# Retention and a two-layer GELU network on one core: seven products for half of the first layer in blocks 3 to 6, scans on GpSimd, attention work in the second layer, the last block by halves

## The chip, the cores and the metric

The kernel runs on one core of one Trainium2 chip. The time is that of one execution on the device, in microseconds (us); of several runs the median is given. A profiled execution comes with it, which has a time of its own.

The core has four engines that compute, each with its own queue of instructions, worked off in order: TensorE (PE; its weight loads are PEld and lie under the matmuls), VectorE (DVE), ScalarE (ACT) and GpSimd (POOL). SyncE (SP) has the queue from which nearly all transfers start. Engines wait for each other through semaphores.

## The reference

Inputs are `q`, `k`, `v` of 8 batches, 8 heads, 576 positions and 64 values a head, and the weights `w_in` (512 x 2048) and `w_out` (2048 x 512), all float32.

```python
def _attn_ref(q, k, v):
    scores = scale * np.matmul(q, k.transpose(0, 1, 3, 2))
    Dmat = np.where(rel >= 0, gamma[:, None, None] ** rel[None, :, :], 0.0)
    return np.matmul(scores * Dmat[None], v)

def _moe_ref(x, w_in, w_out):          # x: 4608 tokens of 512
    h = x @ w_in
    g = 0.5 * h * (1.0 + np.tanh(c * (h + 0.044715 * h * h * h)))
    return g @ w_out
```

Here `gamma` is one decay for each head and `rel` the distance of two positions. The heads of one position, side by side, are one token of the second function.

## The kernel before, in words

**Attention.** A batch's 576 positions are four chunks of 128 and a tail of 64. Tails of two batches are worked on as a pair. Inside a chunk the scores are multiplied by a mask (`score`, then `masks` on DVE) and by v (`av`). What earlier chunks contribute goes through a state: `state` makes a chunk's k-v products in PSUM, `scan` adds them to the state so far and multiplies by a decay (two DVE operations, the first without the addition), `spread` copies the result as float16 into a tile that `past` multiplies with q (`tbd` for chunks, `tbt` for tails). `put` copies a finished chunk from PSUM into `xT`, the network's input.

**Network.** Tokens go in nine blocks of 512, numbered 0 to 8: blocks 0 to 7 are the chunks of one batch each, block 8 holds all the tails. While block t is in the network, the attention of batch t+1 is computed and, from `xT`, block t+1 is built. Batches 0 to 2 are turned by TensorE; from batch 3 on (`NPE = 3`) POOL scales and casts q and k (`cast`), and a DMA transposes them.

A block has a first layer (`up`: 16 plain tiles, each four matmuls of 512 columns, then a GELU on ACT into `gT`) and a second layer. The second layer is done, from block 1 on, as a two-by-two product with **seven products** instead of eight: `prod(t, m, u)` is product m (1 to 7) for half u of the tokens, 8 matmuls of 256 columns. It needs sums of activations (`act_sums`, on DVE, both inputs in SBUF) and of weights (`weight_sums`, made once). `after(t, m, u)` combines products on DVE and stores them. They stand in the order 1, 6, 5, 7, 2, 4, 3, each with two halves; products that share a bank of PSUM (`opA`, `opB`, `opC`) wait until the one before is read. Product 4 writes `opB` after product 7's add has read it.

In blocks 7 and 8 (`WIN`) three quarters of the first layer also go by seven products. `up_prod(t, j, m)` is product m of group j, four matmuls of 256 columns; a group stands for four plain tiles. Its results are copied or added on ACT and DVE before the GELU. `in_sums` makes sums of `w_in` for a group (four DVE operations, in block 6), `x_sums` sums of a block's tokens (four DVE operations). `W_ORDER` is the order of the steps: "12" is product 2 of group 1, "p" a plain tile, "a" activation sums, "Q" product 1 of the second layer. The seventh of a group, say "07", waits for ACT's copy of the sixth.

**Order.** It is written out by hand. A block is a row of steps, numbered u; `at(t, u, f)` puts f behind step u of block t. Steps 0 to 15 are the first layer, 16 to 29 the second. `put`, `scan`, casts and loads hang on such places. A place sets the order in each engine's queue, and nothing else.

**Loads** go to a ring of 16 buffers of 256 KB (`ld`, `LD`). A cast frees a buffer and `pump` then issues the next load of a fixed list. From step 16 of a block until step 29 loads are held back. `gate` is a small POOL copy that waits for the last activation sum, so that POOL's casts begin behind it. `lt` are three buffers of their own for the tails.

## Time and profile before

| | us |
|---|---|
| median of 3 runs | 296.65 (296.27 to 297.05) |
| profiled execution | 296.39 |
| its span | 294.7 |
| PE busy | 282.2 (96%) |
| DVE busy | 191.7 (65%) |
| ACT busy | 168.4 (57%) |
| POOL busy | 100.2 (34%) |

The granted TensorE clock has a mean of 0.997. The span runs from the first instruction to the last; the slices in the profile cut it into 40 equal parts of 7.4 us and give the busy share of each in tenths. In a line of a timeline stand the start in us, the length in us, the engine, the line of the kernel, the operation, output and inputs by name, the shapes, and how many operations are merged; in brackets the idle time before and what ended it. Matmuls are pipelined, so the mean of one (379 ns for 512 columns) is longer than the distance from one to the next. The lengths of single operations also overlap a little on the other engines.

### The profile page before, as it was taken

The page shows a single profiled execution, that of the slowest core. Times are in us where ns is not written, and L with a number is a line of the kernel's source. Part 1 is how long each engine was busy: PE and PEld are TensorE (multiplying, and loading weights), DVE is VectorE, ACT ScalarE, POOL GpSimd, SP SyncE. Part 2 cuts the span into 40 slices and gives each one's busy share as a digit, 9 for nine tenths or more (in the row PEclk, how much of TensorE's full clock was granted, in tenths as well). Part 3 has the DMA queues.
Part 4 walks back from the last instruction along what each step waited for, and adds up shares of the span by engine and source line. Part 5 has one row for each costly group of instructions (what it writes and reads, how often), then busy time and mean ns, then how long its engine had stood idle before and what let it go on. Part 6 is the DMA issues. An engine that isn't in the chain of part 4 may idle for free. (4 is left out here: it accounts for less than half of the span.)

```text
span 294.7 us, 7531 instructions
## 1 busy us (share of the span) xinstructions
PE 282.2 (96%) x3100; PEld 204.3 (69%) x3100; DVE 191.7 (65%) x396; ACT 168.4 (57%) x313; POOL 100.2 (34%) x133
## 2 busy tenths in 40 slices
PE   6779999999999999999999999999999999999993
PEld 2458745888884588448844885478547887887782
DVE  6790606789754873477448654855488968974863
ACT  5377443998239663866386736664666258507800
POOL 4587487960880082007700640059030000000000
PEclk9999999999999999999999999999999999999998
DMA  7999999999969998999899949944941030003013
GB/s 202 307 357 372 341 317 292 280 280 211 194 165 232 216 225 169 261 214 194 103 271 221 169 88 273 211 109 76 263 93 38 0 145 1 2 20 125 1 38 107
DMA packets 129058, 52.92 MB, mean 180 GB/s; under 512 B 101632, under 2 KB 120576, under 8 KB 129024
## 3 DMA queue, kind: packets, MB, share of 16 engines
q1 hardware_dynamic: 128544, 51.92, 74.5%
q8 instruction: 24, 0.39, 0.6%
q10 hardware_dynamic: 480, 0.52, 0.6%
q14 instruction: 10, 0.08, 0.1%
HBM read 36.70 MB, written 9.44 MB: 157 GB/s over the span
## 5 line engine op out<-in xcount | busy, mean ns | idle before, releaser
L471 PE MATMUL hp<-xT,w_in_sb 128*128 128x512 f16 x352 | 79.0, 379 | 0.0
L477 ACT ACTIVATE gT<-hp 128x512 f16<-128x512 f32 x88 | 50.6, 597 | 31.0 <-PE hp L471 30.4
L471 PEld LDWEIGHTS <-w_in_sb 128*128 128x128 f16 x352 | 34.0, 98 | 38.2
L666 PEld LDWEIGHTS <-gT 128*128 128x128 f16 x512 | 49.0, 98 | 7.2 <-issue 0.5
L666 PEld LDWEIGHTS <-s 128*128 128x128 f16 x384 | 37.1, 98 | 4.8
L645 DVE TENSOR_TENSOR s<-gT 128x512 f16<-128x512 f16 x32 | 14.4, 449 | 28.0 <-ACT gT L477 27.0
L953 POOL COPY gate<-s 128x1 f16<-128x1 f16 x5 | 0.9, 190 | 90.7 <-DVE s L649 90.7
L489 PE MATMUL hp<-xT,w_in_sb 128*128 128x256 f16 x256 | 30.3, 273 | 1.1 <-POOL w_in_sb L745 0.9
L666 PE MATMUL opA<-w_out_sb,gT 128*128 128x256 f16 x256 | 31.0, 273 | 0.1
L425 ACT CAST tbd<-ws 64x256 f16<-64x256 f32 x48 | 19.4, 405 | 16.0 <-DVE ws L416 15.4
L489 PEld LDWEIGHTS <-w_in_sb 128*128 128x128 f16 x256 | 24.5, 98 | 4.9 <-POOL w_in_sb L745 1.6
L666 PE MATMUL opB<-wt,gT 128*128 128x256 f16 x224 | 26.9, 273 | 0.1
L383 DVE TENSOR_TENSOR ret<-st,cm 128x512 f16<-128x512 f32 x40 | 24.8, 681 | 0.0
L266 POOL TENSOR_TENSOR cq<-ld,sc 128x512 f16<-128x512 f32 x20 | 21.7, 1086 | 0.0
L460 ACT CAST xT<-xs 128x512 f16<-128x512 f32 x36 | 19.3, 592 | 3.3 <-PE xs L450 1.8
L266 POOL TENSOR_TENSOR ck<-ld,sc 128x512 f16<-128x512 f32 x20 | 21.0, 1050 | 0.0
L495 ACT ACTIVATE gT<-hp 128x512 f16<-128x512 f32 x32 | 18.5, 602 | 3.8 <-PE hp L489 3.5
L680 DVE TENSOR_TENSOR k<-k,opB 128x512 f32<-128x512 f32 x16 | 11.0, 687 | 14.2 <-ACT k L696 7.5
L711 ACT COPY ost<-opA 128x512 f32<-128x512 f32 x8 | 4.7, 586 | 24.1 <-PE opA L666 17.5
L293 ACT COPY tt<-tr 128x1024 f16<-128x1024 f16 (+1 forms) x12 | 11.8, 998 | 10.8 <-PE tr L287 10.7
L416 DVE TENSOR_TENSOR ws<-vs,gt 128x256 f32<-128x256 f32 x24 | 15.7, 654 | 1.1
L666 PE MATMUL opC<-wt,s 128*128 128x256 f16 x128 | 15.5, 273 | 0.0
(124 smaller groups left out, 440.0 us busy)
## 6 DMA issues: line engine op xcount, KB each, us to landing
ld<-in_q_dram SPq DMA_DIRECT2D x32, 256.0 KB, 5.3
ld<-in_k_dram SPq DMA_DIRECT2D x32, 256.0 KB, 5.3
ld<-in_v_dram SPq DMA_DIRECT2D x32, 256.0 KB, 5.4
out_dram<-ost SPq DMA_DIRECT2D x16, 512.0 KB, 3.8
ld<-in_moe_w_in_dram SPq DMA_DIRECT2D x16, 256.0 KB, 5.9
ld<-in_moe_w_out_dram SPq DMA_DIRECT2D x16, 256.0 KB, 5.3
lt<-in_k_dram SPq DMA_DIRECT2D x8, 128.0 KB, 5.4
lt<-in_q_dram SPq DMA_DIRECT2D x8, 128.0 KB, 4.3
```

Of the source, the lines that this page charges most:

```text
L266: eng.tensor_tensor(out=dst.rearrange("p (h d) -> p h d", d=D), in0=raw.rearrange("p (h d) -> p h d", d=D), in1=sc[:, s0].unsqueeze(2).to_ ...
L293: cp(out=o, in_=t)
L383: nc.vector.tensor_tensor(out=r.rearrange("p (n i) -> p n i", i=128), in0=t.rearrange("p (n i) -> p n i", i=128), in1=(cm if b < PAIR else ...
L416: nc.vector.tensor_tensor(out=w, in0=uc, in1=gt, op=ALU.mult)
L425: cp(out=(tbd[b % 2][r, c, :, r] if c < NC - 1 else tbt[b % NT4][r, :, r]), in_=w[r])
L460: nc.scalar.copy(out=xT[:, g0 : g0 + 2], in_=xs.rearrange("p (n g t) -> p g n t", n=HP, g=2))
L471: nc.tensor.matmul(hp.rearrange("p (g t) -> p g t", t=TL), w_in_sb[:, ct, 128 * fc : 128 * fc + 128], xT[:, o : o + TB // TL, ct, :], star ...
L477: nc.scalar.activation(out=gT[t][:, fc].rearrange("p i n -> p (i n)"), in_=hp, func=AF.Gelu_apprx_tanh)
L489: nc.tensor.matmul(hp[:, 256 * x : 256 * x + 256].rearrange("p (g t) -> p g t", t=TL), w_in_sb[:, ct, 128 * (f + x) : 128 * (f + x) + 128] ...
L495: nc.scalar.activation(out=gT[t][:, f : f + 2, 2 * u : 2 * u + 2, :].rearrange("p f i n -> p f (i n)"), in_=hp.rearrange("p (f n) -> p f n ...
L645: nc.vector.tensor_tensor(out=s["1"], in0=a21, in1=a22, op=ALU.add)
L666: nc.tensor.matmul(op[tag][:, HD * u : HD * u + HD], lhs(f), rhs[:, f], start=(new and f == 0), stop=(f == NH - 1), skip_group_check=True,)
```

## The change

- **Blocks 3 to 6:** groups 0 and 1 of the first layer, half of it, go by seven products; `WIN` is 2 there. The other half stays plain. The order of steps is a new entry of `W_ORDER`. Two groups of `in_sums` move from block 6 to block 2; `x_sums` for the next block stands behind step 28.
- **Scans:** from batch 3 on, `take` copies the state from PSUM to SBUF on ACT, and `scan` and `spread` run on POOL, at other places.
- **Scores and masks** of blocks 3 to 6 stand in the second layer: behind steps 16 and 21 instead of 9 and 19; the tails' behind 7 and 11.
- **Last block:** both halves of product 4, then of product 2, then products 6, 5, 7, 3 for the first half of the tokens and again for the second, each with its own banks and adds of 256 columns (`prod_last`, `after_last`). Each half of the tokens is stored as it is done.
- **Memory:** the ring has 18 buffers, of which 7 are kept for sums once batch 2 is loaded; temporaries share the tags of the second layer's. The first weight sum, `wt["1"]`, is written over its own input and moves to block 1.
- **Activation sums** are cut into three parts instead of two, so that they can be placed apart. The hold on loads begins one cast later.

```diff
-    LD = 16
+    LD = 18
+    KEPT = 7
...
+        if b == NPE - 1:
+            seq += [("keep",)] * KEPT
...
+    def take(b, *cs):
+        a = att[b]
+        us = a["U", cs[0]][0]
+        t = sb.tile([128, 512], F32, tag="uc", name="uc", bufs=2)
+        nc.scalar.copy(out=t, in_=us)
+        drop(us)
+        for n, c in enumerate(cs):
+            a["U", c] = (t, n, False)
+
-    def scan(b, c):
+    def scan(b, c, eng=None):
+        eng = eng or nc.vector
...
-            nc.vector.tensor_tensor(out=s, in0=uc, in1=a["w"], op=ALU.add)
+            eng.tensor_tensor(out=s, in0=uc, in1=a["w"], op=ALU.add)
...
-        nc.vector.tensor_tensor(out=w, in0=uc, in1=gt, op=ALU.mult)
+        eng.tensor_tensor(out=w, in0=uc, in1=gt, op=ALU.mult)
...
-    WIN = {t: 3 for t in (NTB - 2, NTB - 1)}
+    FIN = (NTB - 2, NTB - 1)
+    WIN = {t: 3 if t in FIN else 2 for t in range(NPE, NTB)}
...
+    wt["1"] = W12
...
+    def prod_last(t, m, u, lhs, rhs):
+        tag = {6: "B", 7: "B", 5: "C", 3: "E"}[m] + str(u)
+        new = tag not in op
+        if new:
+            op[tag] = bank("op" + tag)
+        for f in range(NH):
+            nc.tensor.matmul(op[tag][:, 0:HD], lhs(f), rhs[:, f], start=(new and f == 0), stop=(f == NH - 1), skip_group_check=True)
+
+    def after_last(m, u):
...
+        elif m == 6:
...
+            add(keep["u2"][:, u], keep["s1"][:, u], acc("B"))
+            if u == 0:
+                for f in range(0, NH, 2):
+                    act_sums(NTB - 1, f, f + 2, parts=(2,))
+            add(keep["u3"][u][:, 0], keep["s1"][:, u], half("D"))
...
+        elif m == 5:
+            add(keep["u3"][u][:, 1], keep["s1"][:, u], acc("C"))
+            add(keep["u2"][:, u], keep["u2"][:, u], acc("C"))
+            drop(op.pop(f"C{u}"))
+        elif m == 7:
+            add(
+                keep["o1"][:, u].rearrange("p (c d) -> p c d", c=2), keep["u3"][u],
+                acc("B").unsqueeze(1).to_broadcast([128, 2, HD]),
+            )
+            drop(op.pop(f"B{u}"))
+            store(keep["o1"][:, u], 1)
+            if u == 1:
+                store(keep["o0"][:, u], 0, slice(0, HD))
+        else:
+            add(keep["o0"][:, u, HD:DM], keep["u2"][:, u], acc("E"))
+            drop(op.pop(f"E{u}"))
+            store(keep["o0"][:, u], 0, slice(0 if u == 0 else HD, DM))
...
     def later(b, c):
-        scan(b, c)
-        spread(b, c, A.copy)
+        eng = P if b >= NPE else V
+        scan(b, c, eng)
+        spread(b, c, P.tensor_copy if b >= NPE else A.copy)
...
-    W_ORDER = (
-        "01 02 05 11 06 12 p 15 07 16 21 22 p 04 25 17 03 26 14 p 13 27 p Q0 24 a0 23 a1 Q1 a3 a2"
-    ).replace("p", "").split(" ")
-    for n in range(GW):
-        at(NTB - 3, 17 + 2 * n, lambda n=n: in_sums(n, (3, 2)))
-        at(NTB - 3, 18 + 2 * n, lambda n=n: in_sums(n, (4, 1)))
-    at(NTB - 3, 27, lambda: x_sums(NTB - 2))
-    at(NTB - 2, 17, lambda: x_sums(NTB - 1))
+    W_ORDER = {
+        2: "01 02 p 05 06 p 11 07 12 p 15 16 04 p 03 17 p a2 b2 p 14 13 a0 b0 p p a1 b1 a3 b3",
+        3: "01 02 05 11 06 12 p 15 07 16 21 22 p 04 25 17 03 26 14 p 13 27 p Q0 24 c0 23 c1 Q1 c3 c2",
+    }
+    for j, (t, u) in enumerate([(NPE - 1, 17), (NPE - 1, 21), (NTB - 3, 24)]):
+        at(t, u, lambda j=j: in_sums(j, (3, 2)))
+        at(t, u if t > NPE else u + 1, lambda j=j: in_sums(j, (4, 1)))
+    for t in WIN:
+        at(t - 1, 17 if t == NTB - 1 else 28, lambda t=t: x_sums(t))
...
+        if t in WIN and t not in FIN:
+            if tl is not None:
+                at(t, 7, lambda t=t, tl=tl: scores(NTB, 0, tl))
+                at(t, 11, lambda t=t, tl=tl: outs(NTB, 0, tl))
+            at(t, 16, lambda t=t, b=b: (scores(t, 0), state(b, 2, 3), take(b, 2, 3)))
+            at(t, 17, lambda b=b: later(b, 2))
+            at(t, 20, lambda t=t: outs(t, 0))
+            at(t, 21, lambda t=t: scores(t, 2))
+            at(t, 26, lambda t=t, nb=b + 1: outs(t, 2, None, (nb, 0, 1) if nb < B else None))
+            at(t + 1, 2, lambda b=b: later(b, 3))
+            for c in range(2 if b + 1 < B else 0):
+                at(t + 1, 4 + 2 * c, lambda c=c, nb=b + 1: later(nb, c))
+            continue
...
-        at(t0, ut[0], lambda: q_ld.update(hold=True))
...
+            if (key, c) == ent[0]:
+                at(t0, u, lambda: q_ld.update(hold=True))
...
+            if t == NTB - 1:
+                two = [(4, 0), (4, 1), (2, 0), (2, 1)] + [(m, u) for u in range(2) for m in (6, 5, 7, 3)]
```

## The prediction

> **What bounds the kernel now.** I read the slices first, then the busy time of each block, then TensorE's timeline inside one block, then the other engines' timelines where the change puts work. The slices say which engine has no air:
>
> ```profile
> PE   6779999999999999999999999999999999999993
> DVE  6790606789754873477448654855488968974863
> ACT  5377443998239663866386736664666258507800
> POOL 4587487960880082007700640059030000000000
> ```
>
> PE is at 9 from the fourth slice to the last but one. Cut at the starts of blocks 2 to 8 (read off PE's timeline):
>
> ```profile
> 87.06:117.61 30.55, 30.55 (x310) 20.94 (x308) 18.93 (x38) 18.75 (x36) 8.98 (x10) 1.00 1.03 214
> 117.61:147.49 29.88, 29.88 (x286) 20.19 (x284) 17.83 (x36) 17.84 (x34) 10.58 (x11) 1.00 0.97 193
> 207.92:238.38 30.46, 30.37 (x295) 20.65 (x293) 24.18 (x53) 16.68 (x32) 2.50 (x2) 1.00 0.34 84
> ```
>
> The columns are the stretch, its length, then busy time of PE, weight loads, DVE, ACT and POOL, then clock and DMA. PE is busy for all of a block, at full clock, so a matmul that goes is time that goes, and a wait that comes is time that comes. The price of both kinds of first-layer step stands in the chain of block 7, which already has the seven products:
>
> ```profile
> 240.72 0.44 PE hA L561 x4
> 241.16 0.86 PE hp L471 x4
> ```
>
> A plain tile (four matmuls of 512 columns) is 0.865 us, a product (four of 256) 0.437. The third thing to see is what DVE pays for an operation with both inputs in SBUF while POOL runs:
>
> ```profile
> 59.32 1.27 DVE L645 TENSOR_TENSOR s<-gT 128x512 f16<-128x512 f16 x1
> 60.62 1.15 DVE L646 TENSOR_TENSOR s<-s,gT 128x512 f16<-128x512 f16 x1
> 61.70 0.83 DVE L647 TENSOR_TENSOR gT<-gT 128x512 f16<-128x512 f16 x1
> 62.45 0.83 DVE L649 TENSOR_TENSOR s<-gT,s 128x512 f16<-128x512 f16 x1
> ```
> ```profile
> 59.08 2.42 POOL L258 TENSOR_TENSOR ck<-ld,sc 128x512 f16<-128x512 f32 x2
> 61.45 1.56 POOL L255 CAST cv<-ld 128x512 f16<-128x512 f32 x2
> ```
>
> Each DVE operation ends where a POOL operation ends: the four take 3.96 us (59.32 to 63.28). With POOL idle the same four take 1.46 (64.27 to 65.83). Operations that read PSUM do not pay: the masks of block 2, in the middle of POOL's casts, stay at 0.6 us each.
>
> **The change part by part.** *Products in blocks 3 to 6.* Each block drops 8 plain tiles (8 x 0.865 = 6.92 us) and gains 14 products (14 x 0.437 = 6.12): 0.80 a block, **-3.2 us** over four. Weight loads stay under the matmuls (98 ns against 109). New beside them, per block: ACT copies of PSUM, 4 x 0.58; DVE, 8 x 0.69 to combine and 4 x 0.42 for the token sums; the GELUs keep their number.
>
> *Scans to POOL.* From batch 3 on, DVE loses 7 operations a batch (3.8 us in block 3), ACT loses 8 spreads (3.3 us) and gains two 0.59 us copies that bring the state to SBUF. DVE goes from 17.8 to about 21.2 us of some 29, ACT from 17.8 to about 18.3, POOL from 8.5 to about 14.5 (its halves of 1.04 and 0.60 us, an estimate). In sum nobody overtakes PE; waits are then a matter of place.
>
> *Block 2: eight weight sums among the casts.* Twelve weight sums stood in block 6, where POOL was idle. Eight of them now stand in block 2's second layer, where POOL makes eight casts of 1.04 us. The first four fall in a gap: DVE has finished the activation sums at 104.1 and waits until 107.2 now, and the scan that filled part of it is gone. The second four stand between the masks and the add that frees bank opB:
>
> ```profile
> 107.84 2.48 DVE L383 TENSOR_TENSOR ret<-st,cm 128x512 f16<-128x512 f32 x4
> 111.20 0.69 DVE L680 TENSOR_TENSOR k<-k,opB 128x512 f32<-128x512 f32 x1 [0.89 <-PE opB L666]
> ```
> ```profile
> 113.76 0.42 PE L399 MATMUL us<-cv,ck 128*64 128x64 f16 x16
> 114.11 1.92 PE L666 MATMUL opB<-wt,gT 128*128 128x256 f16 x16
> ```
>
> The masks end at 110.1 (their add starts at 107.05: the copy it waits for is no longer behind the spreads). If the four sums cost the contended 3.96, the add (0.69) ends at 114.8 and product 4, due at 114.11, waits 0.7 us. If all four meet the wide casts (1.21 each, the mean of 1.27 and 1.15) it is 115.6 and 1.5. Free of contention they take 1.5 and nothing waits; four at 1.37 (a whole cast and 0.33 of its own) make 2.2. I take the middle of the two contended rows, **+1.1** (0 to 2.2).
>
> *The seam between blocks.* Token sums for the next block come after product 4's add, and POOL's scans of the last chunk and the next two run at about that time, since on POOL they wait only for their data. From the end of product 4 to the seventh product of the new block PE has 5.66 us of work: the two halves of product 3 (1.75), two plain tiles (1.73), products 1, 2, 5 and 6 of the first group (1.75) and product 1 of the second (0.44). What product 7 waits for is a copy on ACT behind a GELU, behind a DVE add, behind the token sums: 0.2 + 0.61 + 1.46 + 0.61 + 0.65 + 0.05 + 0.54 + 0.46 + 0.06 = 4.64. POOL's operations are half as wide here, so contention adds half of 2.5: 5.89, a wait of 0.23; with nothing hidden (four at 0.9) 0.7 or so. I take 0.1 a seam, **+0.4** over four (0 to 2.8): nearer to the free row, because scan and spread depend on each other and leave gaps.
>
> A rule of the Trainium skill bears on it (Perfetto Trace Analysis, Optimizing Scalar/DVE Operations; SBUF — State Buffer, Who interferes with whom): work moved between GpSimd and DVE might not help, since a DVE instruction with two SBUF inputs and a GpSimd one that reads SBUF exclude each other for a whole instruction. The rows at 59 us agree (1.27 where 0.42 is usual). Taken to the letter, with every token sum excluded, it gives the upper ends above and the second rival below.
>
> *Second layer of blocks 3 to 6.* Scores now start after the first half of product 1 instead of amid the first layer. DVE then has, without a break: the last eight activation sums (0.34 each), four masks (2.4), an add (0.65), four masks (2.4), an add. Counted from the end of the first layer, with ACT's last GELU at +1.0, the masks end at 5.9 and the values that need the second pair are due at 5.8; the later add ends at 10.8 and product 4 is due at 11.0. I take **+0.2** in all; 0 to 1 from these margins. In the kernel before, the same adds wait 0.4 to 2.7 us for their product, so there was air.
>
> *Loads.* Seven buffers leave the ring: 11 stay for a batch of 12, and the last load goes out only after the first cast. The casts take 1.04 us each and a load lands 5.3 us after issue; the last chunk is cast 6 us or more after the first. The loads of the tails queue behind it on SP; their casts come last on POOL. The transposes go out about 2 us later with POOL's scan ahead of them, but their scores stand 7 to 9 steps later. Cost nothing; the cover is that distance.
>
> *Last block by halves.* PE's work is equal. Product 4 (both halves) fills the 0.28 us hole at 279.83 to 280.11, where product 2 waited for ACT's copy. But DVE gets 16 operations instead of 11 from product 6 on: four sums 1.4, ten adds at 0.35 to 0.42, two at 0.69. Laid behind the products, the last add ends about 290.3 as now (290.34). The last stores have 512 KB behind them where 768 KB went out from 289.3 on. **-0.2** (-0.5 to +0.9). Eight weight sums fewer in block 6 return the 0.09 of idle there, **-0.1**. The start and blocks 0 and 1 keep their waits: two more buffers do not help a queue that waits for its DMAs (5 us of SP's waits on the weight loads name a load), and the one sum (0.69 us) that moves to block 1 stands ahead of activation sums that end at 74.1 and are due when the second half of product 6 begins, 75.1.
>
> **Sum** against the profiled execution's 296.39 (294.7 span and 1.7 around it): -3.2 + 1.1 + 0.4 + 0.2 - 0.2 - 0.1 = -1.8, 294.6. That execution lies 0.26 under the median of 296.65, so in medians **294.8**.
>
> **The rivals.**
> 1. *All is hidden*: POOL's casts and DVE's sums miss each other, as they do where the gate holds POOL back. For it: PE idles 0.1 us in the whole of blocks 2 to 6. Against: in block 2 the order leaves the sums no place outside the casts. 1.1 + 0.4 + 0.2 fall away: 293.1.
> 2. *Exclusion everywhere*: block 2 at 1.5, seams at 0.5 each (between the 0.23 and the 0.7), 0.3 in the second layer: -3.2 + 1.5 + 2.0 + 0.3 - 0.3 = +0.3, 296.9; with 0.4 a seam and 0.2 it is -0.2, 296.4, which I take for this case. No change that can be told.
> 3. *Slower*: in blocks 3 to 6 the DVE chain of the second layer is late at its start. Place: the wait of product 6 for the last activation sums, or of product 4 for opB. ACT's queue sets it: 16 GELUs at 0.55 to 0.60 and four copies in 13.0 us of first layer leave it one or two microseconds. If ACT ends the layer L later than the 1.0 us I counted, each block loses L less 0.2: from L = 0.9 us on the loss of four blocks, 2.8, outweighs the 1.8 and the bound of 0.3%; at 1.3 us the time is 294.8 + 4.4 = 299.2, at 1.0 it is 298.0. Against: block 7 does twelve such GELUs and six copies with PE at 25.97 of 25.97.
>
> **How the numbers follow.** The forecast (293.9 to 295.9) 0.46, rival 1 0.19, rival 2 0.21, rival 3 0.14. The range runs from 293.1 to 297.2, which leaves out most of rival 3 and the lower edge of rival 1. About 0.3% (0.9 us) is what a measurement can tell from no change: faster takes most of the forecast and rival 1, 0.61; within it, rival 2 and the forecast's upper end, 0.26; slower 0.13.
>
> **What would show it.** In the changed kernel: blocks 3 to 6 near 29.1 us with PE full (29.9 without the tails' work before); a PE gap of about a microsecond at product 4 of block 2, released by DVE, with weight sums of 1.2 us in front; token sums over 0.5 us at the seams; the last DVE add within 0.5 us of PE's end plus 0.4. Wrong if PE waits at the first half of product 6 in each block (rival 3), if the weight sums of block 2 last 0.42 (rival 1), or if product 7 waits at each seam (rival 2).

## The result, and the profile after

The changed kernel takes 299.60 us (299.17 to 301.44, six runs) against 296.63 of the kernel before (296.27 to 297.05, six runs): a ratio of 1.010 (1.008 to 1.013), 3.0 us slower. The forecast was 294.8 with a range to 297.2. It is wrong in sign and outside its range.

The profiled execution of the changed kernel took 301.44, one of its longer ones. Its second layer of block 1 starts at 74.58 us; in a second profile of the same kernel it starts at 72.83, and in the kernel before at 72.46, so about 1.8 us of the 5.0 between the two spans belong to the start of that execution alone, where its clock was at half from 20.3 to 23.7 us. What stands behind the start is the same in both profiles of the changed kernel to 0.05 us a block. I therefore compare the kernels by TensorE's stretch from the first matmul of block 1's second layer to the last matmul of all: 217.4 us before, 220.6 after (both profiles). That is 3.2 us, all of the 3.0 that the medians show.

The slices of the profile after (engine, then the busy share of 40 slices in tenths):

```profile
PE   6779998999999998999999999999999999999993
DVE  6780505589753888778578956795689867975874
ACT  5357624998336553486358545753485248607810
POOL 4677387880695059704991399039922600000000
```

VectorE and POOL are fuller in the middle, as the change says. TensorE, which had a 9 in every slice from the fourth to the last but one, has two 8s now; in the second profile of this kernel only the second is left, the slice of block 2's longest wait. The blocks of that execution (stretch, its length, then busy time of PE, weight loads, DVE, ACT and POOL, then clock and DMA):

```profile
89.77:121.45 31.68, 30.61 (x311) 20.98 (x309) 23.32 (x42) 16.91 (x30) 17.66 (x25) 1.00 0.93 188
121.45:151.03 29.58, 29.41 (x310) 22.63 (x308) 21.19 (x42) 17.40 (x32) 16.47 (x23) 1.00 1.02 202
151.03:182.26 31.23, 30.52 (x334) 23.26 (x332) 23.51 (x44) 18.40 (x34) 18.78 (x28) 1.00 0.87 179
...
212.18:243.68 31.50, 30.45 (x319) 22.99 (x317) 25.56 (x49) 15.84 (x29) 13.47 (x22) 1.00 0.44 99
```

Only block 3 became shorter (29.88 before, 29.58 after). Block 2 is 1.1 us longer, block 4 0.7, block 6 1.0; block 5, left out here, is where it was (29.92). The list of TensorE's waits (what waits, for whom: us in total, times, longest) names three new ones; none of the three stands in the list of the kernel before:

```profile
PE opB L705 <- DVE k L781: 1.7, 2, 1.1
PE hB L592 <- ACT wv L621: 1.6, 3, 0.7
PE xs L474 <- DVE ret L395: 0.7, 3, 0.4
```

The list counts a wait after the matmul in flight has drained. Laid out by the distance between the starts of neighbouring matmuls, less what the matmul itself takes, the loss is a little larger, and there is one kind that the list does not know at all. I use this measure from here on:

| place | before | after |
|---|---|---|
| block 1, product 7 waits for VectorE's add | 0.19 | 0.80 |
| block 2, product 4 waits for VectorE's add | 0 | 1.23 |
| blocks 3, 4, 5, 6: product 7 of group 0 waits for ScalarE's copy | 0 | 0, 0.87, 0.34, 0.87 |
| blocks 3, 4, 5, 6: values wait for VectorE's masks | 0 | 0.34, 0, 0.34, 0.52 |
| blocks 3, 4, 5, 6: gaps of 0.09 to 0.10, nobody waited for | 8, 8, 8, 7 (the eighth is part of the hole below) | 9, 13, 9, 13 |
| block 6, one hole | 0.26 | 0 |

Product 7 below is the one of group 0 in the first layer, unless block 1 or the second layer is named with it.

Plain tiles and products cost what the profile before said. In the timeline of TensorE at the start of block 3 (start, busy, engine and line, tile):

```profile
121.88 0.60 PE L592 MATMUL hA<-xT,w_in_sb 128*128 128x256 f16 x4
122.32 1.03 PE L495 MATMUL hp<-xT,w_in_sb 128*128 128x512 f16 x4
123.18 0.60 PE L592 MATMUL hC<-wk,w_in_sb 128*128 128x256 f16 x4
```

A product starts 0.44 us ahead of its neighbour, a plain tile 0.86. So the gain came, and it was given back, with interest, in the five places of the table.

**Block 2.** The last three of the second four weight sums, on VectorE (the first took 0.93), and one of POOL's casts at the same time:

```profile
113.80 1.15 DVE L545 TENSOR_TENSOR wk<-wk,w_in_sb 128x512 f16<-128x512 f16 x1
114.97 1.15 DVE L545 TENSOR_TENSOR wk<-w_in_sb,wk 128x512 f16<-128x512 f16 x1
116.05 1.26 DVE L545 TENSOR_TENSOR w_in_sb<-w_in_sb 128x512 f16<-128x512 f16 x1
117.23 0.67 DVE L781 TENSOR_TENSOR k<-k,opB 128x512 f32<-128x512 f32 x1
```
```profile
115.81 1.22 POOL L278 TENSOR_TENSOR cq<-ld,sc 128x512 f16<-128x512 f32 x1
```

One sum a cast, and the casts pay too (1.22 where 1.04 is their time alone). The add that frees bank B begins at 117.23, and product 4 starts right behind it at 117.96 with `[1.06 <-DVE k L781]`.

**The seam from block 3 to block 4.** VectorE's token sums, what POOL does then, and the product that waits:

```profile
150.09 0.42 DVE L559 TENSOR_TENSOR wk<-xT 128x512 f16<-128x512 f16 x1
150.54 1.15 DVE L559 TENSOR_TENSOR wk<-wk,xT 128x512 f16<-128x512 f16 x1
151.62 0.95 DVE L559 TENSOR_TENSOR wk<-xT 128x512 f16<-128x512 f16 x1
152.49 0.94 DVE L559 TENSOR_TENSOR wk<-xT,wk 128x512 f16<-128x512 f16 x1
```
```profile
149.16 2.25 POOL L278 TENSOR_TENSOR e<-lt,sc 128x512 f16<-128x512 f32 x2
151.38 0.91 POOL L437 TENSOR_TENSOR uc<-uc,ws 128x256 f32<-128x256 f32 x1
```
```profile
155.81 0.60 PE L592 MATMUL hB<-wk 128*128 128x256 f16 x4 [0.70 <-ACT wv L621]
```

The second sum meets the casts of the tails, the third and fourth meet the scan of the last chunk. The wait is named after ScalarE, but ScalarE is only the last link: its copy stands behind a GELU that waits for a VectorE add that stands behind these sums. One figure shows that. Counted from the start of the block, VectorE is through with the four sums (the operation behind them starts) at +1.40 us in block 3 (wait 0), at +1.79 in block 5 (0.34) and at +2.32 in block 4 (0.87): in these three seams, what lies beyond +1.45 is paid in full.

**Block 1.** The moved sum is the second of the two in the first line below; behind it come the last activation sums, and then the scan of chunk 2, whose second half meets POOL's first cast:

```profile
74.77 1.28 DVE L669 TENSOR_TENSOR w_out_sb<-w_out_sb 128x1024 f16<-128x1024 f16 x2
77.89 1.17 DVE L440 TENSOR_TENSOR ws<-vs,gt 128x256 f32<-128x256 f32 x1
80.55 0.69 DVE L781 TENSOR_TENSOR k<-k,opB 128x512 f32<-128x512 f32 x1 [1.49 <-ACT k L789]
```

In the kernel before, that half of the scan met a cast as well:

```profile
75.18 1.16 DVE L416 TENSOR_TENSOR ws<-vs,gt 128x256 f32<-128x256 f32 x1
```

So the cast is not what is new. Counted from the start of the second layer (72.46 before, 74.58 after), this operation starts at 3.31 us instead of 2.72: the whole chain is 0.59 later, and the wait at product 7 goes from 0.19 to 0.80.

**The gaps that no engine causes.** TensorE's timeline at the first visit of the attention in block 3's second layer; the field with the asterisk is the part of the array (rows by columns) that a matmul uses:

```profile
134.47 1.04 PE L705 MATMUL opA<-w_out_sb,gT 128*128 128x256 f16 x8
135.44 0.62 PE L386 MATMUL st<-tt 64*128 64x128 f16 x16
135.99 0.44 PE L411 MATMUL us<-cv,ck 128*64 128x64 f16 x16
136.36 1.05 PE L705 MATMUL opA<-w_out_sb,gT 128*128 128x256 f16 x8
137.25 1.91 PE L705 MATMUL opB<-wt,s 128*128 128x256 f16 x16
```

Sixteen matmuls of 256 columns take 1.74 us where the next matmul is of the same kind (137.25 to 138.99, the start of product 5), so eight take 0.87. The first eight here take 0.97 until the scores start, the second eight 0.89. At each step between 128\*128, 64\*128 and 128\*64 about 0.1 us is lost. Steps within one kind lose nothing: the values (128\*64) run into the state (128\*64) without a gap, and the past scores (128\*128) start behind a product without one. In the kernel before it is the same: these sixteen take 1.84 until scores start, 0.10 more than 1.74.

```profile
134.98 1.91 PE L666 MATMUL opB<-wt,s 128*128 128x256 f16 x16
136.82 0.62 PE L374 MATMUL st<-tt 64*128 64x128 f16 x16
```

TensorE's weight loads (PEld) in the kernel after, around the visit above:

```profile
135.43 0.45 PEld L386 LDWEIGHTS <-tt 64*128 64x128 f16 x16 [0.21 <-issue]
136.36 0.77 PEld L705 LDWEIGHTS <-gT 128*128 128x128 f16 x8
137.14 0.42 PEld L705 LDWEIGHTS <-s 128*128 128x128 f16 x4
```

Within one kind a load begins 0.11 us ahead of its matmul, while the matmul before runs (137.14 for the product at 137.25). At a change of kind none begins until the gap is over (135.43 for the scores at 135.44, 136.36 for the product that also starts at 136.36). What holds the load back the trace does not say.

### The profile page after: what moved, and what is told of

The parts are those of the page before. It is cut to its first block, busy times and chain, and to the rows that moved or that the text cites. A ratio compares the mean times of both kernels' runs of the same rounds, so it can differ in the third digit from the quotient of the medians.

```text
span 299.7 us, 7849 instructions
## 1 busy us (share of the span) xinstructions
PE 283.4 (95%) x3196; PEld 214.9 (72%) x3196; DVE 208.9 (70%) x414; ACT 165.0 (55%) x299; POOL 141.6 (47%) x208
## 4 chain that ended last, share of the span: by engine, by line
PE 60%; DVE 19%; DMA 10%; SPq 4%; ACT 3%; issue 2%; POOL 1%; POOLq 0%; ACTq 0%; DVEq 0%
PE hp L495 12%; PE opB L705 9%; PE hB L592 7%; PE opA L705 6%; PE opC L705 5%; DMA ld<-in_moe_w_in_dram 4%; PE hC L592 4%; SPq L103 3%; DVE ret L395 3%; DMA ld<-in_q_dram 2%; DVE s L682 2%; PE xs L474 2%; PE hA L592 2%; DMA ld<-in_moe_w_out_dram 2%; DVE s L686 2%
## 5 line engine op out<-in xcount | busy, mean ns | idle before, releaser
L705 PEld LDWEIGHTS <-gT 128*128 128x128 f16 x496 | 47.0, 98 | 9.9 <-issue 1.8
L495 PE MATMUL hp<-xT,w_in_sb 128*128 128x512 f16 x224 | 53.9, 379 | 0.0
L501 ACT ACTIVATE gT<-hp 128x512 f16<-128x512 f32 x56 | 32.8, 593 | 9.7 <-PE hp L495 9.6
L495 PEld LDWEIGHTS <-w_in_sb 128*128 128x128 f16 x224 | 21.8, 98 | 19.3
L705 PEld LDWEIGHTS <-s 128*128 128x128 f16 x336 | 32.4, 98 | 4.3
L513 PEld LDWEIGHTS <-w_in_sb 128*128 128x128 f16 x256 | 25.0, 100 | 6.0 <-POOL w_in_sb L835 2.2
L592 PEld LDWEIGHTS <-w_in_sb 128*128 128x128 f16 x224 | 21.9, 98 | 6.8
L705 PE MATMUL opC<-w_out_sb,s 128*128 128x256 f16 x208 | 25.7, 273 | 0.0
L437 POOL TENSOR_TENSOR uc<-uc,ws 128x256 f32<-128x256 f32 x15 | 11.5, 767 | 24.1 <-issue 13.2
L519 ACT ACTIVATE gT<-hp 128x512 f16<-128x512 f32 x32 | 18.5, 602 | 5.3 <-PE hp L513 5.0
L592 PEld LDWEIGHTS <-wk 128*128 128x128 f16 x168 | 16.0, 98 | 5.4 <-issue 2.1
L265 ACT CAST cv<-ld 128x512 f16<-128x512 f32 x19 | 11.3, 620 | 15.1 <-DMA ld<-in_v_dram 15.1
L592 PE MATMUL hB<-wk 128*128 128x256 f16 x112 | 16.5, 272 | 1.6 <-ACT wv L621 1.6
```

Of the source, the lines that this page charges most:

```text
L265: eng.copy(out=dst, in_=raw)
L437: eng.tensor_tensor(out=s, in0=uc, in1=a["w"], op=ALU.add)
L495: nc.tensor.matmul(hp.rearrange("p (g t) -> p g t", t=TL), w_in_sb[:, ct, 128 * fc : 128 * fc + 128], xT[:, o : o + TB // TL, ct, :], star ...
L501: nc.scalar.activation(out=gT[t][:, fc].rearrange("p i n -> p (i n)"), in_=hp, func=AF.Gelu_apprx_tanh)
L513: nc.tensor.matmul(hp[:, 256 * x : 256 * x + 256].rearrange("p (g t) -> p g t", t=TL), w_in_sb[:, ct, 128 * (f + x) : 128 * (f + x) + 128] ...
L519: nc.scalar.activation(out=gT[t][:, f : f + 2, 2 * u : 2 * u + 2, :].rearrange("p f i n -> p f (i n)"), in_=hp.rearrange("p (f n) -> p f n ...
```

## The experiments

My theory after the trace: TensorE's 3.2 us are really saved, and 5 to 6 are lost in five places with four causes: VectorE's sums beside POOL's reads (block 2 and the seams), VectorE's masks behind its own sums, the sum moved to block 1, and more steps between kinds of matmul. The rivals were, by place, that something else is late there (ScalarE's queue, a bank, the loads), and for the whole, that the scans on POOL or the start are to blame. Times are medians; the kernel before stood at 296.8 to 297.0 on the chips of these runs. Where a run is compared with the changed kernel, that is its second run, 299.84 us with a stretch of 220.6.

### The changed kernel again

No edit.

> The changed kernel again, to have its profile beside the others. In the profile of its first execution block 0's first layer was 1 us longer and the start 1.2 us later than in the kernel before, at a granted clock of 0.994 over the span. If that belonged to that execution alone, a span of 297 to 298 us and these two differences under 0.3 us are expected; if the later start belongs to the change (the longer ring of load buffers), both stay. In either case TensorE's waits behind block 1 should come back place by place: 0.6 to 0.8 us at product 7 of block 1, 1.2 at product 4 of block 2, 0.9, 0.3 and 0.9 at product 7 of the first group in blocks 4, 5 and 6, 0.3 to 0.5 at the values of blocks 3, 5 and 6.

299.84 us, a ratio of 1.010 (1.007 to 1.013); the span of its profile is 298.0. The second layer of block 1 starts 0.4 us later than before, not 2.1: the start belonged to the first execution. Every wait came back at its place within 0.01 us.

### POOL's scans behind the token sums

```diff
+            at(t + 1, 2, lambda t=t: nc.gpsimd.tensor_copy(out=gate, in_=xw[4][:, 3, 1, TL - 1 : TL]))
             at(t + 1, 2, lambda b=b: later(b, 3))
```

> One copy of 128x1 is added on POOL ahead of the scans of the seam, in blocks 4 to 7: it reads the last token sum, so POOL's scans begin when the token sums are done. Theory (the sums pay for POOL's reads): the token sums that met the scans fall from 0.94 to 0.42 us, the sums end 1.0 to 1.5 us earlier, the waits of product 7 of group 0 (0.87, 0.34 and 0.86 in blocks 4, 5 and 6) fall to 0.3 in all, and the time falls by 1.5 to 2.0 us; the second token sum of blocks 4 and 6 stays at 1.15, since it meets the casts of the tails and not a scan. Rival (the copy on ACT is late because of ACT's own queue): the sums fall and the waits stay, within 0.3 us. Rival (the scans may not be late): the state that they make is then missing at the second pair's past scores, and the time rises.

297.42 us, ratio 1.001 (0.999 to 1.003): 2.4 less than the changed kernel. The stretch is 218.6, 2.0 less. All three waits of product 7 are gone, also the one in block 4, whose second token sum stays beside the casts of the tails (1.15). The token sums of block 5:

```profile
178.36 0.42 DVE L559 TENSOR_TENSOR wk<-xT 128x512 f16<-128x512 f16 x1
...
179.49 0.42 DVE L559 TENSOR_TENSOR wk<-xT,wk 128x512 f16<-128x512 f16 x1
```

They took 0.87, 0.50, 0.61 and 0.94 at this seam in the changed kernel. One copy of a column on POOL removes 2.1 us of waits: the cause at the seams is shown, and the scans have room to be later. The rivals (ScalarE's own queue; the scans may not be late) fall.

### Block 2's weight sums in its first layer

```diff
-    for j, (t, u) in enumerate([(NPE - 1, 17), (NPE - 1, 21), (NTB - 3, 24)]):
-        at(t, u, lambda j=j: in_sums(j, (3, 2)))
-        at(t, u if t > NPE else u + 1, lambda j=j: in_sums(j, (4, 1)))
+    for j in range(2):
+        at(NPE - 1, 1 + 4 * j, lambda j=j: in_sums(j, (3, 2, 4)))
+        at(NPE - 1, 17, lambda j=j: in_sums(j, (1,)))
+    at(NTB - 3, 24, lambda: in_sums(2, (3, 2, 4, 1)))
```

> Six of the eight weight sums of block 2 go from its second layer to its first, where POOL does nothing; the two that write over the weights in use stay in the second layer, ahead of the casts of POOL. Theory (sums beside casts cost 0.9 to 1.3 us instead of 0.42, and the add that frees bank B stands behind them): the wait at product 4 of block 2, 1.2 us, falls to 0.1 or less; the six sums take 0.42 each, and the time falls by 1.0 to 1.2 us. Rival (the wait is for the casts themselves, or for a bank that is freed late by something else): the wait stays over 0.6 us.

298.62 us, ratio 1.006 (1.004 to 1.007): 1.2 less than the changed kernel. Block 2 is back at 30.56 us, its length before. The second three of the moved sums, beside an idle POOL:

```profile
93.30 0.41 DVE L545 TENSOR_TENSOR wk<-w_in_sb 128x512 f16<-128x512 f16 x1
...
94.21 0.42 DVE L545 TENSOR_TENSOR wk<-w_in_sb,wk 128x512 f16<-128x512 f16 x1
```

The stretch fell by 0.9 only, because a wait of 0.19 came up at product 7 of block 3: block 2's delay had given the token sums of that seam the time that they lacked.

### Block 1's sum in a gap of VectorE

```diff
-    at(1, 14, lambda: weight_sums(0, [0], V))
+    at(1, 5, lambda: weight_sums(0, [0], V))
```

> The weight sum that was moved to the end of block 1's first layer (0.69 us on VectorE) goes to the middle of that layer, where VectorE waits 1.0 us for a GELU. Theory (that sum holds up the last activation sums, the scan behind them meets the first cast of POOL, and ScalarE's spread and copy come late): the wait of 0.6 to 0.8 us at product 7 of block 1 falls to 0.2 or less and the time falls by 0.5 to 0.7 us. Rival (the add there waits for ScalarE's copy of another bank, whatever VectorE does): no change within 0.2 us.

298.81 us, ratio 1.007 (1.004 to 1.010): 1.0 less than the changed kernel, of which the stretch explains 0.5 (220.2). The wait at product 7 falls from 0.80 to 0.32. The theory holds for the larger part; the expected "0.2 or less" was missed, and the rest is the scan that still meets POOL's cast ahead of ScalarE's copy.

### The masks ahead of the last sums

```diff
-        2: "... a2 b2 p 14 13 a0 b0 p p a1 b1 a3 b3",
+        2: "... a2 b2 p 14 13 a0 b0 p p a1 a3",
...
-            at(t, 16, lambda t=t, b=b: (scores(t, 0), state(b, 2, 3), take(b, 2, 3)))
+            at(t, 16, lambda t=t, b=b: (scores(t, 0), [act_sums(t, f, f + 2, parts=(1, 2)) for f in (2, 6)], state(b, 2, 3), take(b, 2, 3)))
```

> In blocks 3 to 6 the last four activation sums (the differences that products 7 and 3 need) go behind the first four masks of the second layer on VectorE; until now they stood ahead of them, 0.34 us each. Theory (the masks are late because VectorE has eight sums ahead of them): the masks end 1.4 us earlier, the waits of the values, 0.34, 0.34 and 0.52 us in blocks 3, 5 and 6, go, and the time falls by 1.0 to 1.2 us; the gate of POOL, which reads one of these sums, lets POOL's casts begin 2.4 us later, which costs nothing if what they make is not due. Rival (the masks wait for TensorE's scores, which come late): no change within 0.3 us. Rival (the sums become late for product 7, which starts six steps after the scores, or the casts for their transposes): new waits of 0.3 us or more a block and no gain.

305.26 us, ratio 1.027 (1.022 to 1.032): 5.4 more than the changed kernel. The waits of the values are gone, as the theory said, and the forecast was still 6 us off: the clause "which costs nothing" was false. POOL's casts, let go 2.4 us later, run into all four token sums of the next block. The seam from block 3 to block 4, first VectorE, then POOL, then TensorE:

```profile
147.93 1.17 DVE L559 TENSOR_TENSOR wk<-xT 128x512 f16<-128x512 f16 x1
149.13 1.15 DVE L559 TENSOR_TENSOR wk<-wk,xT 128x512 f16<-128x512 f16 x1
150.20 1.26 DVE L559 TENSOR_TENSOR wk<-xT 128x512 f16<-128x512 f16 x1
151.38 1.26 DVE L559 TENSOR_TENSOR wk<-xT,wk 128x512 f16<-128x512 f16 x1
```
```profile
149.96 2.40 POOL L278 TENSOR_TENSOR e<-lt,sc 128x512 f16<-128x512 f32 x2
```
```profile
155.02 0.60 PE L592 MATMUL hB<-wk 128*128 128x256 f16 x4 [2.08 <-ACT wv L621]
```

The sums end at +3.69 us in the block, and the wait is 2.25: on the same line as the three seams above (1.45 us free, then one for one). In blocks 5 and 6 it is 1.27 and 2.25, so the three seams lose 3.7 us more than in the changed kernel. The rest is in block 6: about 1.6 us by a clock that falls to half behind the wait (see the last section), and 0.8 at product 7 of the second layer, because the two last sums (1.26 each) meet the casts of the tails and the add behind them frees its bank. Less the 1.2 of the values this is 4.9, where the stretch is 4.7 longer.

### The gate of the casts read from an earlier sum

The edit above, and with it:

```diff
-        at(t0, ut[0], lambda t=t0: nc.gpsimd.tensor_copy(out=gate, in_=gs[t]["4"][:, NH - 1, 1, 0:1]))
+        at(t0, ut[0], lambda t=t0: nc.gpsimd.tensor_copy(out=gate, in_=gs[t]["4" if t < NPE else "2"][:, NH - 1, 1, 0:1]))
```

> The masks ahead of the last four sums, as before, but the gate of POOL's casts in blocks 3 to 5 reads a sum that is made ahead of these masks, so that the casts begin about 1.5 us earlier than in the changed kernel instead of 2.4 later. Theory (the 5 us that the masks edit cost came from the gate alone: the casts ran on into the token sums of the next block, 1.15 to 1.26 each instead of 0.42): the token sums fall to 0.4 to 0.6 with none beside a 1.04 us cast, so the waits of product 7 fall from 2.25, 1.27 and 2.25 to under 0.4 each; the waits of the values stay away; the four sums behind the masks now meet casts (about 1.1 each), which delays the add of product 6 by 2 us and may cost up to 0.5 a block at product 4. Time 296.5 to 298. Rival (sums behind the masks are late whatever POOL does): 300 or more, with TensorE waiting for sums in the second layer.

298.88 us, ratio 1.007 (1.006 to 1.009). Against the kernel above, 6.4 us come back by moving the start of POOL's casts alone (5.3 by the stretch, with the 1.6 of the clock among them), and the waits of product 7 fall to 0.28, 0 and 0.28: the late gate was the cause of that kernel's loss at the seams. The time itself missed the expected range by 0.9. What was put at "up to 0.5 a block at product 4" came at product 7 of the second layer instead and was larger, 0.71, 0.37, 0.79 and 0.88 in blocks 3 to 6: its bank is freed by the add behind the four sums. TensorE's list of waits has only that line left of the second layers (1.7 of it in blocks 1 and 2):

```profile
PE opB L705 <- DVE k L781: 3.8, 6, 1.1
```

So the rival was right for the second layer: masks first moves the wait from the values to the next bank.

### More visits of the attention

```diff
-            at(t, 16, lambda t=t, b=b: (scores(t, 0), state(b, 2, 3), take(b, 2, 3)))
-            at(t, 17, lambda b=b: later(b, 2))
+            at(t, 16, lambda t=t: scores(t, 0))
+            at(t, 18, lambda b=b: (state(b, 2, 3), take(b, 2, 3)))
+            at(t, 19, lambda b=b: later(b, 2))
...
-            at(t, 21, lambda t=t: scores(t, 2))
-            at(t, 26, lambda t=t, nb=b + 1: outs(t, 2, None, (nb, 0, 1) if nb < B else None))
+            at(t, 21, lambda t=t, b=b: (score(b, 2), masks(b, 2)))
+            at(t, 22, lambda t=t, b=b: (score(b, 3), masks(b, 3)))
+            at(t, 26, lambda t=t: outs(t, 2))
+            if b + 1 < B:
+                at(t, 27, lambda nb=b + 1: (state(nb, 0, 1), take(nb, 0, 1)))
```

> In the second layer of blocks 3 to 6 the same matmuls of the attention are spread over more places: the state of the second pair of chunks is taken out of the visit with the first scores, the second pair's scores are cut in two, and the state for the next batch stands one product behind the outputs (not in block 6, which has none). No matmul is added. Theory (TensorE loses 0.09 to 0.10 us each time it goes from matmuls with whole 128x128 weights to matmuls on half of the rows or columns, or back): about five more switches a block in blocks 3 to 5 and three in block 6, 18 x 0.1 = 1.8 us more, found in the trace as gaps of 0.09 to 0.10 us at the new places, with no engine named as what TensorE waits for. Rival (the gaps are the wait for a bank or for data that is just in time, and belong to the old places): the gaps do not multiply, and the time stays within 0.4 us.

299.74 us, ratio 1.010 (1.008 to 1.013): the time did not move. The gaps did what the theory said: 14, 18, 14 and 16 in blocks 3 to 6 instead of 9, 13, 9 and 13, each of 0.09 to 0.10 us, 1.7 us more in sum. The scores that are now two visits, in block 3:

```profile
139.69 0.40 PE L386 MATMUL st<-tt 64*128 64x128 f16 x8
140.02 1.05 PE L705 MATMUL opB<-wt,gT 128*128 128x256 f16 x8
141.00 0.40 PE L386 MATMUL st<-tt 64*128 64x128 f16 x8
```

Eight matmuls of a product take 0.98 here until the next visit. The gaps were paid out of other waits: product 7 of group 0 now waits 0, 0.41, 0 and 0.41 instead of 0, 0.87, 0.34 and 0.87, because the state and with it POOL's scans came later, and the values wait nowhere; for these 2.5 us it gave 1.7 in gaps and 0.8 in new waits inside product 6 (0.23, 0.23 and 0.32 in blocks 3, 5 and 6). The price of a step is shown; the total was a coincidence, which the forecast of 1.8 us missed.

### Blocks 3 to 6 by plain tiles, the rest of the change kept

```diff
-    WIN = {t: 3 if t in FIN else 2 for t in range(NPE, NTB)}
+    WIN = {t: 3 for t in FIN}
```

The plain tiles here read the first-layer weights after block 2's sums have overwritten a part of them, so the output isn't the reference's; the work of every engine is as described.

> Blocks 3 to 6 have their first layer by plain tiles again (56 products out, 32 plain tiles in), with the places of scores and outputs that the kernel before had; everything else of the change stays: the scans on POOL, block 1's sum, the eight weight sums in block 2, the loads, the last block by halves. Theory (3.2 us of TensorE's work are really saved, and 2.1 at the seams, 1.2 at the values and 1.2 in switches of matmul kind are lost in the same four blocks): the waits of product 7 and of the values go, block 2's 1.2 and block 1's 0.8 stay, the blocks 3 to 6 are as long as in the kernel before within 0.1 us each, and the time is 298.2, about 1.4 under the changed kernel. Rival (the scans on POOL or the shorter ring of load buffers cost by themselves, whatever the first layer does): waits in blocks 3 to 6 stay, and the time is 299.5 or more.

297.60 us, ratio 1.003 (1.002 to 1.004): 2.2 less than the changed kernel, 1.7 by the stretch (219.0). Block 3:

```profile
119.86:149.74 29.88, 29.88 (x287) 20.15 (x285) 14.30 (x29) 16.00 (x28) 16.59 (x24) 1.00 1.02 199
```

Blocks 3, 4 and 5 are as long as in the kernel before to 0.01 us, with eight gaps and no wait; blocks 1 and 2 keep theirs (0.79 and 1.23). So in these blocks the scans on POOL, the copies of the state and the shorter ring of loads cost nothing by themselves. The products together with what had to move for them cost 1.7 to 2.2 us where 3.2 were to be gained.

### The scans back on VectorE and ScalarE

```diff
     def later(b, c):
-        eng = P if b >= NPE else V
-        scan(b, c, eng)
-        spread(b, c, P.tensor_copy if b >= NPE else A.copy)
+        scan(b, c, V)
+        spread(b, c, A.copy)
...
     def take(b, *cs):
+        return
...
-            at(t + 1, 2, lambda b=b: later(b, 3))
+            at(t, 27, lambda b=b: later(b, 3))
...
-                at(t + 1, 4 + 2 * c, lambda c=c, nb=b + 1: later(nb, c))
+                at(t + 1, c, lambda c=c, nb=b + 1: later(nb, c))
```

> The scans of batches 3 to 7 are back on VectorE, their spreads on ScalarE, at the places of the kernel before, and the two copies of the state by ScalarE are gone; the products of blocks 3 to 6 and everything else stay. Theory (the engines beside TensorE are short of room once the products' own work is there): ScalarE, which has 16 GELUs and four copies of some 0.6 us in 13.0 us of first layer, gets up to six spreads of 0.4 us on top of them, VectorE seven operations of 0.4 to 0.5; token sums at the seams are at 0.42 again, but copies and GELUs are late by 1 us or more a block, and the time is 301 or more. Rival (the scans on POOL are what costs, and without them the change gains): the waits of the seams go as with the copy on POOL, and the time is 297.5 or less.

324.96 us, ratio 1.093 (1.089 to 1.096). The token sums are at 0.42 again, and it is 25 us worse:

```profile
PE st L386 <- ACT xT L485: 7.6, 8, 2.0
PE hB L593 <- ACT wv L622: 7.2, 4, 2.3
```

Product 7 waits 2.0 to 2.5 us a block for ScalarE, behind spreads, and the scores wait for a bank that ScalarE frees. The theory's direction holds, but its "301 or more" was far too mild, and the granted clock (at half for five stretches of 3.4 us, which is at most 8.5 of the 25) and an order that was not made for this kernel have a part in it. What it shows: the seams' loss cannot be had back by undoing the scans.

### The four edits together

The scans behind the token sums, block 2's sums, block 1's sum and the masks first.

> The four edits together: the scans behind the token sums, the weight sums of block 2 in its first layer, block 1's sum in the gap, and the masks ahead of the last sums. If they are independent: 299.6 less 2.4, 1.2, 0.5 and 1.2 is 294.3, under the kernel before by 2.3 (ratio 0.992). Rival (they share VectorE: the masks' gain puts sums or casts where another edit put its work, or the seam from block 2 to block 3, which has no copy on POOL, now waits because block 2 does not): 295.5 or more.

300.82 us, ratio 1.013 (1.010 to 1.016), where 294.3 would be the sum. The masks edit brings its late casts along: product 7 waits 2.25 in block 4 and 2.24 in block 6 although the scans are held back, since it is casts and not scans that meet the sums, and block 6 loses the clock and the 0.8 at product 7 of the second layer here too. The edits are not independent.

### Without the masks edit, the values half a product later

The three edits that worked, the copy on POOL at the seam from block 2 to 3 too, block 1's scan behind ScalarE's copy, and:

```diff
-    at(1, 16, lambda: later(2, 2))
+    at(1, 18, lambda: later(2, 2))
...
-            at(t, 20, lambda t=t: outs(t, 0))
-            at(t, 21, lambda t=t: scores(t, 2))
+            at(t, 21, lambda t=t: outs(t, 0))
+            at(t, 22, lambda t=t: scores(t, 2))
```

> Together: POOL's scans behind the token sums (at the seam from block 2 to 3 too), block 2's six weight sums in its first layer, block 1's sum in the gap of VectorE, block 1's scan of chunk 2 behind ScalarE's copy instead of ahead of it, and in blocks 3 to 6 the first pair's values and the second pair's scores half a product later instead of masks ahead of sums. The gate of POOL's casts stays where it was. From the start of block 1's second layer to the last matmul the changed kernel takes 220.6 us, the kernel before 217.4. Theory: less 2.0 (seams), 1.2 (block 2), 0.5 and 0.3 (block 1), 1.0 to 1.2 (values): 215.4, so 294.5 us, ratio about 0.993. Rival (a wait goes only to come back at the next place, as it did when the masks were put first): 217 or more, 296.5 us or more; the place would be product 4 of each block, for whose bank VectorE's add then comes half a microsecond later.

296.12 us, ratio 0.998 (0.995 to 1.000). The stretch is 217.3, against the theory's 215.4 and the rival's 217. Block 2, the seams and the values (but for 0.22 and 0.37 in block 6) are clean, and product 7 of block 1 waits no more. A wait of 0.38 a block is new, at product 4, for the add that frees bank B: as the rival said, with the scores later, so are masks and add.

### The same, with values and scores in one visit

```diff
+            at(t, 21, lambda t=t: (outs(t, 0), scores(t, 2)))
```

in place of the two lines.

> The same, but the second pair's scores stand directly behind the first pair's values, in one visit of the attention. Theory on the switches of matmul kind: one visit less a block saves 0.1 to 0.2 us a block, 0.4 to 0.8 in all against the kernel with two visits. Rival (the scores need four banks at once, and banks of the values are freed only by ScalarE): TensorE waits between values and scores, 0.3 us or more a block, and it is slower than with two visits.

295.01 us, ratio 0.993 (0.990 to 0.996): 1.8 us under the kernel before and 4.8 under the changed kernel. The stretch is 216.0. The waits at product 4 are gone, there are 8, 12, 8 and 12 steps between kinds instead of 9, 13, 9 and 13, and the rival's wait is there too, 0.23 amid the scores of blocks 3, 4 and 5. Blocks 3 and 4:

```profile
118.12:147.50 29.38, 29.31 (x311) 22.67 (x308) 20.44 (x41) 17.29 (x32) 18.19 (x27) 1.00 1.02 204
147.50:178.00 30.50, 30.43 (x335) 23.34 (x332) 22.63 (x45) 18.40 (x34) 17.11 (x26) 1.00 0.88 185
```

Block 3 has eight gaps as in the kernel before and one wait of 0.23, and is 0.50 shorter: the products are worth 0.73 there, against the 0.80 counted. Block 4 is only 0.06 shorter: four more gaps (0.38) and a wait of 0.23 eat the rest.

## Why the prediction was wrong, step by step

**The products, -3.2.** Right: 0.73 of 0.80 is seen in block 3 of the last experiment. What the step left out is that the change also moves the attention. Scores and values of the tails, which stood in one visit with others, stand alone in blocks 4 and 6, which makes four steps more in each; and in every block the state stands behind scores, of another kind, and no longer behind values, of its own. That is 9, 13, 9 and 13 gaps between kinds of matmul instead of 8, 8, 8 and 7, 13 x 0.095 = **+1.2**, for which the sum has no term. The kernel before already showed the price: 0.10 us at each such step. The working's "weight loads stay under the matmuls" holds within one kind and fails just there.

**Block 2, +1.1.** Right in place, mechanism and size: 31.67 against 30.56, with sums of 0.93 to 1.26, and gone when POOL is idle beside them.

**The seam, +0.4, measured 2.1.** The largest of the mis-sized terms. The path was counted well: 5.66 less 4.64 leaves 1.02 us of air for free sums; in the experiment with the copy on POOL, VectorE is through with free sums at +0.52 in block 5, and the limit is +1.45, so it has 0.93. (Its 1.46 for four free sums is the distance from the first start to the next operation, 178.36 to 179.82 in that experiment; the two ends that it gives, 64.27 and 65.83, are 1.56 apart.) The step's own price for half contention, a wait of 0.23, is near what block 5 shows (0.34). The error is the choice of 0.1, "nearer to the free row, because scan and spread depend on each other and leave gaps": what they left was too short: beside a scan a sum took 0.86 to 0.95, beside a spread 0.50 to 0.62. The other error is in "POOL's operations are half as wide here": in blocks 4 and 6 the casts of the tails, full width, are still on POOL then, and the wait is 0.87, above the 0.7 that was the case of nothing hidden. The loads' step had put these casts "last on POOL" at no cost; the cover that it named was the distance to their scores, and the neighbour that they met was another. The rule of the Trainium skill that the prediction weighed (SBUF — State Buffer, Who interferes with whom) was right, and the trace agrees: 0.42 alone, 1.15 to 1.26 beside a cast of 1.04.

**The second layer, +0.2, measured 1.2.** The masks were put at 5.9 us behind the first layer's end against 5.8 for the values that need them: a margin of -0.1 in a block, called air. Measured in block 3, the masks end at 6.2 and the values were due at 6.0; with the signal between the engines that made 0.34. The eight sums took 2.94 instead of 2.7, because the second of each four starts 0.45 us behind the first that it reads, not 0.34. A margin that small is no cover.

**"The start and blocks 0 and 1 keep their waits", 0, measured +0.6 in block 1** (35.80 against 35.21; the wait of product 7 went from 0.19 to 0.80). The step asked whether the activation sums would be late for product 6; they are not. It did not follow what is queued behind them: the scan stands behind the sums and now comes 0.59 us later (it meets POOL's first cast as it did before, 1.17 against 1.16), ScalarE's spread waits for the scan, ScalarE's copy of bank A stands behind the spread, and VectorE's add for bank B behind that copy. Product 7, which reuses bank B, already waited 0.19 in the kernel before, so this chain had no slack to give.

**The last block by halves, -0.2; block 6's sums, -0.1.** Right in size; for the first, half of the reason failed. The hole of 0.28 us that product 4 was to fill is still there, 0.26, four matmuls into product 4, which waits for the last GELU, and the last block is as long as before (25.51 against 25.53). The gain is at the stores, which the step had also named: the last add ends 0.46 us behind the last matmul in both kernels, and from the last matmul to the end of the span it is 4.5 us instead of 4.8. The hole of 0.26 in block 6 is gone.

Together: -2.9 for the products (4 x 0.73), +1.2 steps, +2.1 seams, +1.2 values, +1.1 block 2, +0.6 block 1, -0.3 for the end and -0.26 for block 6 make +2.7, against 3.0 in the medians.

**The rivals.** The second, exclusion everywhere, names the main mechanism, but its 296.4 took 0.4 a seam and 0.2 in the second layer. The third, on the slower side, put the loss at product 6 or product 4 of blocks 3 to 6 through a late ScalarE; those did not wait, and its cause did not act: ScalarE ended the layer at +0.8 to +1.15, where the working counted 1.0. That its 299.2 is close to the measured time is luck. The chance of 0.13 for slower was too low: three of the terms (seams, second layer, block 1) stood on a margin of a microsecond or less against something on the critical path (1.0 with free sums and none with contended ones, -0.1, and none at product 7), all taken at the cheap end, and all failed.

## What to carry to other kernels

Where TensorE is busy for all of a block, price the starts and not only the lengths: each time its matmuls change kind it loses a tenth of a microsecond here, and work that is moved out of a shared visit makes two more of them. A sum of two SBUF tiles on VectorE costs two to three times its own time beside POOL's reads, so moving work to POOL is free only where the order keeps the two apart; a one-column copy that makes POOL wait for the last sum was worth 2 us, and a gate that let POOL's casts go 2.4 us later cost 5, a third of it by the clock. Follow a late instruction past its first reader, through the queue of every engine that it holds up, until a chain ends in slack that you have measured.

## What the hardware did that I had not expected

TensorE's price for a change of kind is the same wherever it stands: 0.09 to 0.10 us between any two of 128\*128, 64\*128 and 128\*64, in every kernel of this study, and nothing within one kind. The Trainium skill (TensorEngine Tiling (Array Packing), Key Properties) says that a change of tiling mode drains the engine; the traces agree in that each such change costs time and a step within one mode none.

POOL's operations of half the width (128x256, f32) take 0.72 to 0.73 us alone, not half of the 1.04 of a 128x512 one, as the prediction estimated; a spread of 64x256 takes 0.40, where it had 0.30.

A wait can cost the clock, and where it lies decides whether it does. In all 14 traces every full stretch of one granted clock, from 3.41 to 290.1 us long, is a whole multiple of 3.41 us: the clock is set anew on a grid of that width. Cut along this grid, between the first matmul of block 1's second layer and the last of all, TensorE was idle for 1.94 to 2.33 us in seven windows, and each of these was followed by one at half clock; in the other windows, some 890 of them, it was idle for 1.75 us or less, and none was. Two waits of 2.25 us in the kernel with the masks first show the difference. The one in block 6 lay within a window (2.08 us idle), and 3.41 us at half clock followed. The one in block 4 lay across an edge (0.62 us idle ahead of it, 1.47 behind), and the clock stayed. At the start of the kernel this border does not hold: there windows with 1.5 to 1.9 us idle were enough in four of the traces.

The Trainium skill (TensorE: Matmul & The Clock Gate, Part 1) has the clock fall after an idle window of about 3.4 us that runs freely. The width of the grid agrees; here a window did not have to be idle all through, about 2 us of it sufficed.
